# A transformer block: rounded keys and queries are stored once, and a pair's load takes them twice

## The chip, the cores and the metric

The kernel runs on one core of a Trainium2 chip. A core has five engines that run side by side, each through its own list of instructions: TensorE (PE, matrix products; PEld is its weight load), VectorE (DVE), ScalarE (ACT), GpSimd (POOL) and SyncE (SP). SP computes nothing: all transfers of this kernel are issued on it, in program order, and are carried out by the core's 16 DMA engines. The metric is the device time of one execution in microseconds (us), as the median of several runs. The profile comes from one more execution, taken by the hardware profiler.

## The reference

The block takes `x` (1 x 2048 x 512), modulates and normalizes it, and adds a gated attention over 32 heads of 16 columns and a gated dense layer with the Mish activation:

```python
mod = (_silu(c) @ w_mod).reshape(c.shape[0], 6, 1, -1)      # sa, ca, ga, sb, cb, gb
h = _layernorm(x) * (1 + ca) + sa
q, k, v = split(h @ wqkv)                                   # 32 heads, 16 columns each
p = softmax((q @ k.T) * 16 ** -0.5)                         # 2048 x 2048 a head
x = x + ga * (concat(p @ v) @ wo)
h = _layernorm(x) * (1 + cb) + sb
x = x + gb * (mish(h @ w1 + b1) @ w2)                       # 512 -> 1792 -> 512
```

All of it is in 32-bit floats.

## The kernel before

PE multiplies in a rounded 32-bit format. To keep the accuracy, a number is split into its rounded part (`qh`, called hi here) and the remainder (`ql`, lo), and a product is taken as hi x hi + hi x lo + lo x hi. For keys and queries this sum is folded into the contraction: 16 columns of a head become 48 rows, in which hi and lo stand in such an order that row by row the three products come out. A head's query rows are hi, hi, lo and its key rows hi, lo, hi, interleaved by column.

The rows are built through memory. `qk_unit` computes 128 columns (8 heads) of queries or keys for a block of 512 positions (`TB`), splits them, and its `put` (lines 266 to 277) stores them to the scratch tensors `qscr` (32 heads x 50 rows x 2048) and `kscr` (32 x 48 x 2048). Rounded rows are written twice there: queries by two transfers, keys by one transfer whose source repeats. Rows 48 and 49 of `qscr` start as zeros (`constants`, line 470) and are replaced in the loaded tile by the negated row maxima, split likewise (`mt`, line 577), so that the product subtracts the maximum.

Attention goes by *pairs* of heads. `load_q` (L313) and `load_k` (L322) bring one pair into one of five tiles `qa` and five tiles `ka`: head 0 into partitions 0 to 49, head 1 into 64 to 113, one transfer a head and operand. A *round* `n` handles 4 heads, pairs `2n` and `2n + 1`, for one block of 512 queries; there are 32 rounds of 16 steps. In each step PE takes products for the maxima of a later round (L539, reduced by DVE at L541), scores of this round (L588, exponentials by ACT at L591) and products with the values (L606), and in between a slice of other work: the projections early on, the dense layer of the block before later (L139). Before the rounds, maxima of the first rounds are taken at L553.

The order is written by hand. A step has two half-steps, and `at(h, f)` hangs a load or a store on half-step `h`. Loads of pairs:

```python
if n > 2: at(32 * (n - 2) + (2 if n in (3, 4, 5, 7) else 15 if n % 2 == 0 else 9), lambda n=n: load_pair(2 * n))
if n > 1: at(32 * (n - 1), lambda n=n: load_pair(2 * n + 1))
```

The maxima run 20 steps ahead of the scores (`PRO`), so the odd pair's tile is first read by L539 some 8 half-steps after its load is due. Its tile becomes free only when the scores that used it are done, which is what SP waits for there. `mt` is sent at half-step 26 of a round of 32, for the scores that begin 6 half-steps later.

SP signals the landing of its transfers on eight semaphores in turn (`DMAHW0` to `DMAHW7`). A transfer is issued only when the one eight places before it on the queue has landed, so at most eight are under way.

Of the kernel before, what the change touches and what calls it, by code (L numbers as in the profile page):

```python
# [8 lines left out]
F32 = mybir.dt.float32  # L9
# [9 lines left out]
def adaln_block(ctx: ExitStack, tc: tile.TileContext, x, wqkv, wo, w1, b1, w2, c, w_mod, out):  # L19
    nc = tc.nc  # L20
    P = 128
    S, D = x.shape[1], x.shape[2]
    F = w1.shape[1]
    H = 32
    DH = D // H
    DK = D // P
    FT = F // P
    TB = 512
# [25 lines left out]
    dram = ctx.enter_context(tc.tile_pool(name="dram", bufs=1, space=DRAM))  # L54
    ps = ctx.enter_context(tc.tile_pool(name="ps", bufs=1, space=PSUM))

    kscr = dram.tile([H, 48, S], F32, name="kscr")
    qscr = dram.tile([H, 50, S], F32, name="qscr")
    vscr = dram.tile([G, P, VROW], F32, name="vscr")
    woscr = dram.tile([DK, P, 2, D], F32, name="woscr")  # L60
    w1scr = dram.tile([FT, P, 2, D], F32, name="w1scr")
# [27 lines left out]
    def dap(t, off, ap):  # L89
        return bass.AP(tensor=t.tensor, offset=t.offset + off, ap=ap)  # L90

    def hi_copy(eng, hi, src):
        if eng == "a":
            nc.scalar.copy(hi, src)
        elif eng == "v":
            nc.vector.tensor_copy(hi, src)
        else:
            nc.gpsimd.tensor_scalar(hi, src, 1.0, 0.0, op0=ALU.mult, op1=ALU.add)  # L98

    def lo_sub(eng, lo, src, hi):  # L100
        (nc.gpsimd if eng == "p" else nc.vector).tensor_sub(lo, src, hi.bitcast(F32))  # L101
# [15 lines left out]
    def mm3(acc, ah, al, bh, bl, late="a"):  # L117

        n = len(ah)
        seq = ((ah, bh), (ah, bl), (al, bh)) if late == "a" else ((ah, bh), (al, bh), (ah, bl))  # L120
        seq = [(l[k], r[k]) for l, r in seq for k in range(n)]
        for i, (l, r) in enumerate(seq):
            mm(acc, l, r, i == 0, i == len(seq) - 1)
# [41 lines left out]
    def bank(tag="ms"):  # L165
        return ring() if tag == "ring" else ps.tile([P, TB], F32, tag=tag, name="bk", bufs=1)
# [25 lines left out]
    def clear(h):  # L192

        return h if h < 60 or h % 32 < 25 else h - h % 32 + 34
# [10 lines left out]
    def at(h, f):  # L205

        hooks.setdefault(h, []).append(f)
# [38 lines left out]
    def qk_unit(kind, ct, tb, tag):  # L246

        wh, wl = slices[kind, ct]
        acc = bank(tag)
        ts_ = slice(tb * TB, (tb + 1) * TB)  # L250
        mm3(acc, [wh[:, k, :] for k in range(DK)], [wl[:, k, :] for k in range(DK)],
            [h_h[:, k, ts_] for k in range(DK)], [h_l[:, k, ts_] for k in range(DK)], "b")

        def fin(h=None):
            qh = qp.tile([P, TB], F32R, tag="qh", name="qh", bufs=2)
            ql = qp.tile([P, TB], F32R, tag="ql", name="ql", bufs=2)
            if h is None:
                hi_copy("a", qh, acc)
                lo_sub("v", ql, acc, qh)
            else:  # L260
                qf = pw.tile([P, TB], F32, tag="raw", name="qf", bufs=1)
                nc.scalar.copy(qf, acc)  # L262
                hi_copy("p", qh, qf)
                lo_sub("p", ql, qf, qh)
            scr, rows = (qscr, 50) if kind == 0 else (kscr, 48)

            def put():
                put_away.add((kind, ct, tb))
                o = 8 * ct * rows * S + tb * TB
                if kind == 0:  # L270
                    for r, src in enumerate((qh, qh, ql)):
                        nc.sync.dma_start(dap(scr, o + r * S, [[rows * S, 8], [3 * S, DH], [1, TB]]), src.bitcast(F32))
                    return
                hi = qh.bitcast(F32)
                twice = bass.AP(tensor=hi.tensor, offset=hi.offset, ap=[list(hi.ap)[0], [0, 2], [1, TB]])
                nc.sync.dma_start(dap(scr, o, [[3 * S, P], [2 * S, 2], [1, TB]]), twice)
                nc.sync.dma_start(dap(scr, o + S, [[3 * S, P], [1, TB]]), ql.bitcast(F32))

            put() if h is None else at(clear(h + (5 if h > 60 else 2)), put)
        return fin  # L280
# [25 lines left out]
    def load_q(pp, rows=50):  # L306
        n, j = divmod(pp, 2)
        qb, g = divmod(n, G)
        h = 4 * g + 2 * j
        qt = qa[pp % NR].bitcast(F32)  # L310
        assert (0, h // 8, qb) in put_away, (pp, put_away)
        for s in range(2):
            nc.sync.dma_start(qt[64 * s:64 * s + rows, :], qscr[h + s, :rows, qb * TB:(qb + 1) * TB])  # L313

    def load_k(pp, tb=None):
        n, j = divmod(pp, 2)
        h = 4 * (n % G) + 2 * j
        kt = ka[pp % NR].bitcast(F32)
        at_ = slice(0, S) if tb is None else slice(tb * TB, (tb + 1) * TB)
        assert {(1, h // 8, i) for i in (range(NB) if tb is None else (tb,))} <= put_away, (pp, put_away)  # L320
        for s in range(2):
            nc.sync.dma_start(kt[64 * s:64 * s + 48, at_], kscr[h + s, :, at_])  # L322

    def load_pair(pp):
        load_q(pp)
        load_k(pp)


    with ExitStack() as es:
# [23 lines left out]
        zer = lp.tile([P, TB], F32, name="zer")  # L353
# [113 lines left out]
        apply_tb(1)  # L467
        def constants():
            for q4 in range(S // TB):
                nc.sync.dma_start(dap(qscr, 48 * S + q4 * TB, [[50 * S, H], [S, 2], [1, TB]]), zer[:64, :])  # L470
            nc.sync.dma_start(dap(vscr, VROW - 16, [[VROW, P], [P * VROW, G], [1, 16]]), zer[:, :16 * G])
            nc.sync.dma_start(b1c, b1.rearrange("(f p) -> p f", p=P))

        def unit(fin):
            pe_run()
            fin()

        constants()
        for tb in range(NB):
            if tb + 2 < NB:  # L480
# [27 lines left out]
            if tb == 0:  # L508
                for pp in range(2):
                    load_q(pp, 48)  # L510
            for pp in range(2):
                load_k(pp, tb)
# [7 lines left out]
    ap = ctx.enter_context(tc.tile_pool(name="ap", bufs=1, reuse_waits="tile"))  # L520
# [1029 lines left out]
```

## Time and profile before

| | |
|---|---|
| median of 3 runs | 1691.56 us (1690.99 to 1694.38) |
| the profiled execution | 1691.02 us, span 1689.2 us |
| PE busy | 1667.3 us |
| pair loads | 124 of keys, 384 KB each; 124 of queries, 100 KB each |
| DMA, mean | 141 GB/s, 238.98 MB |
| written to memory | 51.45 MB |

The span runs from the first instruction to the last. Times in rows are in us from the span's start, unless marked ns. In a row of a timeline stand start, duration, engine, line, operation, and what it writes and reads; `SPq` rows are the issuing of transfers, not their running. In a row of windows stand the stretch, its length, busy time of PE, PEld, DVE, ACT and POOL with counts of instructions, the clock granted to PE as a share, the mean busy share of the 16 DMA engines, and the GB/s that they moved.

### The profile page before, as it was taken

What the parts mean: (1) busy time and instruction counts of PE and PEld (TensorE: products, weight loads), DVE (VectorE), ACT (ScalarE), POOL (GpSimd) and SP (SyncE); (2) the same over time, 40 slices, a digit from 0 to 9 for tenths busy, and PEclk for the clock granted to TensorE, in tenths of its full rate; (3) what the DMA queues carried; (4) which work ended last, traced back from release to release, by engine and by line L of the source; (5) the groups of instructions that cost most, each with busy time, mean ns of one, the idle gap of its engine ahead of it and who ended that gap; (6) DMA issues with size and microseconds to landing.
All of it is one profiled execution on the core that took longest, in us unless ns stands there. A gap on an engine that the chain in (4) does not pass through costs nothing.

```text
span 1689.2 us, 33772 instructions
## 1 busy us (share of the span) xinstructions
PE 1667.3 (99%) x12418; PEld 921.5 (55%) x12418; DVE 1441.5 (85%) x2369; ACT 1355.1 (80%) x2612; POOL 821.1 (49%) x843
## 2 busy tenths in 40 slices
PE   7999999999999999999999999999999999999999
PEld 5755655555444455555555455555555455555687
DVE  8898888888989988888889888888889888883377
ACT  6257777777778998888888998888888998889674
POOL 7555224655313564556323564556323565555442
PEclk9999999999999999999999999999999999999999
DMA  7877556777755443434355434534354533533261
GB/s 248 269 244 199 147 150 185 218 223 216 231 142 146 110 94 98 117 88 129 84 137 152 115 77 93 139 77 127 87 144 122 130 94 77 144 107 132 75 230 63
DMA packets 115406, 238.98 MB, mean 141 GB/s; under 512 B 24928, under 2 KB 50544, under 8 KB 109288
## 3 DMA queue, kind: packets, MB, share of 16 engines
q1 hardware_dynamic: 115240, 236.82, 49.9%
q8 instruction: 98, 1.61, 0.4%
q14 instruction: 68, 0.56, 0.1%
HBM read 180.48 MB, written 51.45 MB: 137 GB/s over the span
## 4 chain that ended last, share of the span: by engine, by line
PE 91%; DVE 3%; ACT 3%; DMA 2%; POOL 1%; issue 1%; SPq 0%; ACTq 0%; DVEq 0%; POOLq 0%
PE bk L606 29%; PE ring L588 22%; PE ring L539 20%; PE bk L139 11%; PE bk L132 3%; PE ring L1219 2%; PE ring L132 2%; DVE mx L541 2%; ACT pr L591 1%; PE ring L553 0%; DMA qa<-mt 0%; DMA xt<-in_A_x 0%; PE ring L922 0%; DMA kscr<-qh 0%; PE ring L568 0%
## 5 line engine op out<-in xcount | busy, mean ns | idle before, releaser
L541 DVE TENSOR_REDUCE mx<-ring 128x1 f32<-128x512 f32 x1968 | 1223.1, 682 | 150.0 <-PE ring L539 136.4
L591 ACT ACTIVATE pr<-ring 128x512 f32<-128x512 f32 x2048 | 1078.4, 603 | 207.1 <-PE bk L139 124.7
L539 PE MATMUL ring<-ka,qa 64*128 64x512 f32 x1968 | 817.9, 429 | 1.4 <-ACT pr L591 1.1
L588 PE MATMUL ring<-qa,ka 64*128 64x512 f32 x2048 | 759.1, 402 | 3.4 <-ACT pr L591 1.9
L606 PE MATMUL bk<-pr,vg 128*32 128x512 f32 x4096 | 545.1, 604 | 0.0
L539 PEld LDWEIGHTS ring<-ka,qa 64*128 64x128 f32 x1968 | 350.5, 184 | 326.2 <-DVE mx L541 251.3
L588 PEld LDWEIGHTS ring<-qa,ka 64*128 64x128 f32 x2048 | 373.7, 184 | 194.7 <-DVE mx L541 111.4
L139 PE MATMUL bk<-h,w 64*128 64x512 f32 (+1 forms) x1080 | 278.1, 390 | 0.0
L139 PE MATMUL bk<-w,a_h 64*128 64x512 f32 x632 | 210.9, 413 | 0.0
L139 PEld LDWEIGHTS bk<-h,w 64*128 64x128 f32 x1080 | 178.5, 184 | 9.3 <-ACT pr L591 1.5
L606 PEld LDWEIGHTS bk<-pr,vg 128*32 128x32 f32 x4096 | 81.2, 108 | 135.4 <-issue 126.0
L139 PE MATMUL bk<-w,a_l 64*128 64x512 f32 x316 | 124.0, 392 | 0.0
L139 PEld LDWEIGHTS bk<-w,a_h 64*128 64x128 f32 x632 | 106.8, 184 | 4.3 <-ACT hb L800 1.0
L978 POOL TENSOR_TENSOR y<-yd,y 128x512 f32<-128x512 f32 x44 | 56.9, 1293 | 89.0 <-ACT yd L977 79.7
L812 POOL TENSOR_SCALAR qq<-ee 128x512 f32<-128x512 f32 x25 | 15.5, 619 | 169.6 <-ACT ee L806 169.6
L828 POOL TENSOR_TENSOR qq<-qq,rr 128x512 f32<-128x512 f32 x42 | 54.1, 1289 | 85.9 <-ACT rr L822 85.9
L814 POOL TENSOR_TENSOR hb<-hb,ee 128x512 f32<-128x512 f32 x42 | 54.1, 1288 | 79.6 <-DVE ee L810 77.7
L139 PE MATMUL bk<-w,o_hl 64*128 64x512 f32 x288 | 79.1, 405 | 0.0
L101 POOL TENSOR_TENSOR a_l<-hb,a_h 128x512 fp32r<-128x512 f32 x53 | 73.1, 1379 | 4.4
L98 POOL TENSOR_SCALAR qh<-qf 128x512 fp32r<-128x512 f32 x27 | 16.7, 619 | 90.8 <-ACT qf L262 69.4
L139 PEld LDWEIGHTS bk<-w,a_l 64*128 64x128 f32 x316 | 58.3, 185 | 3.4
L139 PE MATMUL bk<-h_h,wl 64*128 64x512 f32 x168 | 57.2, 420 | 0.2 <-ACT pr L591 0.2
(219 smaller groups left out, 1909.1 us busy)
## 6 DMA issues: line engine op xcount, KB each, us to landing
ka<-kscr SPq DMA_DIRECT2D x124, 384.0 KB
w<-w2scr SPq DMA_DIRECT2D x56, 512.0 KB
w<-w1scr SPq DMA_DIRECT2D x46, 512.0 KB
vg<-vscr SPq DMA_DIRECT2D x32, 552.0 KB
qa<-qscr SPq DMA_DIRECT2D x124, 100.0 KB
kscr<-qh SPq DMA_DIRECT2D x16, 512.0 KB
qscr<-qh SPq DMA_DIRECT2D x32, 256.0 KB
w2scr<-hl SPq DMA_DIRECT2D x14, 512.0 KB
```

The source lines that it names most:

```text
L101: (nc.gpsimd if eng == "p" else nc.vector).tensor_sub(lo, src, hi.bitcast(F32))
L132: nc.tensor.matmul(acc, l, r, start=start, stop=stop)
L139: i = nc.tensor.matmul(acc, l[64 * g:64 * g + 64], r[64 * g:64 * g + 64], start=start and not then, stop=bool(stop and then))
L539: nc.tensor.matmul(pm, qt[64 * s:64 * s + 64, qs * P:(qs + 1) * P], kt[64 * s:64 * s + 64, kb * TB:(kb + 1) * TB], start=True, stop=True)
L541: nc.vector.tensor_reduce(out=mxs[n][:, s, 4 * j + qs, kb:kb + 1], in_=pm, op=ALU.max, axis=AX.X)
L588: nc.tensor.matmul(p_, kt[64 * s:64 * s + 64, kc * P:(kc + 1) * P], qt[64 * s:64 * s + 64, :], start=True, stop=True)
L591: e = nc.scalar.activation(pr, p_, AF.Exp, scale=SCALE)
L606: nc.tensor.matmul(accs[n][32 * h:32 * h + 32, :], vgs[n][:, o:o + 32], pts.pop((t, h)), start=(kc == 0), stop=(kc == 15))
L814: (nc.vector if tail else nc.gpsimd).tensor_mul(hb, hb, ee)
L828: nc.gpsimd.tensor_mul(qq, qq, rr)
L978: nc.gpsimd.tensor_add(y[i], yd, y[i])
L1219: nc.tensor.matmul(po[i // 2][:, i % 2, :], l[:, s], w[:, r, :], start=(f == 0 and j == 0), stop=(f == FT - 1 and j == 2))
```

## The change

Three things change, all in transfers; no other engine's instructions differ.

- **Stores.** `kscr` has 32 rows a head and `qscr` 34: 16 rounded, 16 of the remainder, and for queries the two rows of zeros. Each of `qh` and `ql` is stored once, by one transfer. For queries one transfer of 256 KB goes (16 of them in all); for keys the first transfer shrinks from 512 KB to 256 KB. The memory side of both now counts 8 heads, 16 rows, 512 elements, where that of the keys counted 128 rows.
- **Loads.** The rounded rows are read twice by one transfer, whose source starts with a step of 0 and a count of 2; a second transfer brings the remainder (and for queries the two zero rows). A pair takes eight transfers in place of four.
- **Order of rows.** The rows of a tile are no longer interleaved: queries are 16 hi, 16 hi, 16 lo, keys 16 lo, 16 hi, 16 hi. The 48 products are the same, summed in another order.

```diff
-    kscr = dram.tile([H, 48, S], F32, name="kscr")
-    qscr = dram.tile([H, 50, S], F32, name="qscr")
+    kscr = dram.tile([H, 32, S], F32, name="kscr")
+    qscr = dram.tile([H, 34, S], F32, name="qscr")
...
-                if kind == 0:
-                    for r, src in enumerate((qh, qh, ql)):
-                        nc.sync.dma_start(dap(scr, o + r * S, [[rows * S, 8], [3 * S, DH], [1, TB]]), src.bitcast(F32))
-                    return
-                hi = qh.bitcast(F32)
-                twice = bass.AP(tensor=hi.tensor, offset=hi.offset, ap=[list(hi.ap)[0], [0, 2], [1, TB]])
-                nc.sync.dma_start(dap(scr, o, [[3 * S, P], [2 * S, 2], [1, TB]]), twice)
-                nc.sync.dma_start(dap(scr, o + S, [[3 * S, P], [1, TB]]), ql.bitcast(F32))
+                for r, src in enumerate((qh, ql)):
+                    nc.sync.dma_start(dap(scr, o + r * DH * S, [[rows * S, 8], [S, DH], [1, TB]]), src.bitcast(F32))
...
         for s in range(2):
-            nc.sync.dma_start(qt[64 * s:64 * s + rows, :], qscr[h + s, :rows, qb * TB:(qb + 1) * TB])
+            b, o = 64 * s, (h + s) * 34 * S + qb * TB
+            nc.sync.dma_start(qt[b:b + 32, :], dap(qscr, o, [[0, 2], [S, DH], [1, TB]]))
+            nc.sync.dma_start(qt[b + 32:b + rows, :], dap(qscr, o + DH * S, [[S, rows - 32], [1, TB]]))
...
         for s in range(2):
-            nc.sync.dma_start(kt[64 * s:64 * s + 48, at_], kscr[h + s, :, at_])
+            b, o = 64 * s, (h + s) * 32 * S + at_.start
+            nc.sync.dma_start(kt[b:b + DH, at_], dap(kscr, o + DH * S, [[S, DH], [1, w]]))
+            nc.sync.dma_start(kt[b + DH:b + 48, at_], dap(kscr, o, [[0, 2], [S, DH], [1, w]]))
```

On the SP queue this moves what stands behind a pair's load. First, a place in the middle of the rounds: the load of pair 25 (tiles `qa0`, `ka0`) with the transfers behind it, a weight (`w1`), the sums (`sm`) and the head rows (`od`) of the round just ended; the names in brackets are the semaphores waited for. Before:

```order
L313 DMA qa0_107<-qscr_67 50x512 [waits PE_49]
L313 DMA qa0_107<-qscr_67 50x512 [waits DMAHW2_49]
L322 DMA ka0_105<-kscr_66 48x2048 [waits DMAHW3_49]
L322 DMA ka0_105<-kscr_66 48x2048 [waits DMAHW4_49]
L751 DMA w1_7775<-w1scr_70 128x1024 [waits DMAHW5_49,PE_49]
L631 DMA sm_7773<-ot_7769 128x1x16 [waits DMAHW6_49,Activation_49]
L635 DMA od_7771<-ot_7769 16x512 [waits DMAHW7_49,Pool_49]
```

And with the change, at the same place:

```order
L308 DMA qa0_107<-qscr_67 32x1x512 [waits PE_49]
L309 DMA qa0_107<-qscr_67 18x512 [waits DMAHW2_49]
L308 DMA qa0_107<-qscr_67 32x1x512 [waits DMAHW3_49]
L309 DMA qa0_107<-qscr_67 18x512 [waits DMAHW4_49]
L319 DMA ka0_105<-kscr_66 16x2048 [waits DMAHW5_49]
L320 DMA ka0_105<-kscr_66 32x1x2048 [waits DMAHW6_49]
L319 DMA ka0_105<-kscr_66 16x2048 [waits DMAHW7_49]
L320 DMA ka0_105<-kscr_66 32x1x2048 [waits DMAHW0_49]
L749 DMA w1_7875<-w1scr_70 128x1024 [waits DMAHW1_49,PE_49]
L629 DMA sm_7873<-ot_7869 128x1x16 [waits DMAHW2_49,Activation_49]
```

A pair now takes all eight semaphores, and the weight behind it waits for the pair's own first transfer, `sm` for its second, where before they waited for transfers ahead of the pair.

Second, the start of the rounds, at the load of pair 3 (tiles `qa3`, `ka3`) between two stores of keys. Before:

```order
L276 DMA kscr_66<-qh_990 128x2x512 [waits DMAHW3_49,Pool_49]
L277 DMA kscr_66<-ql_991 128x512 [waits DMAHW4_49,Pool_49]
L313 DMA qa3_110<-qscr_67 50x512 [waits DMAHW5_49]
L313 DMA qa3_110<-qscr_67 50x512 [waits DMAHW6_49]
L322 DMA ka3_631<-kscr_66 48x2048 [waits DMAHW7_49]
L322 DMA ka3_631<-kscr_66 48x2048 [waits DMAHW0_49]
L276 DMA kscr_66<-qh_1011 128x2x512 [waits DMAHW1_49,Pool_49]
L277 DMA kscr_66<-ql_1012 128x512 [waits DMAHW2_49,Pool_49]
```

And with the change, where the first two stores (8x16x512 both) stand as before, from the load on:

```order
L308 DMA qa3_110<-qscr_67 32x1x512 [waits DMAHW3_49]
L309 DMA qa3_110<-qscr_67 18x512 [waits DMAHW4_49]
L308 DMA qa3_110<-qscr_67 32x1x512 [waits DMAHW5_49]
L309 DMA qa3_110<-qscr_67 18x512 [waits DMAHW6_49]
L319 DMA ka3_650<-kscr_66 16x2048 [waits DMAHW7_49]
L320 DMA ka3_650<-kscr_66 32x1x2048 [waits DMAHW0_49]
L319 DMA ka3_650<-kscr_66 16x2048 [waits DMAHW1_49]
L320 DMA ka3_650<-kscr_66 32x1x2048 [waits DMAHW2_49]
L271 DMA kscr_66<-qh_1033 8x16x512 [waits DMAHW3_49,Pool_49]
L271 DMA kscr_66<-ql_1034 8x16x512 [waits DMAHW4_49,Pool_49]
```

The stores behind the pair now wait for transfers of the pair itself. The whole SP queue grows from 1022 to 1274 transfers.

More of the change, by code (lines that the diff above doesn't have):

```diff
@@ L264, in fin @@
                 lo_sub("p", ql, qf, qh)
-            scr, rows = (qscr, 50) if kind == 0 else (kscr, 48)
+            scr, rows = (qscr, 34) if kind == 0 else (kscr, 32)
             def put():
@@ L318, in load_k @@
         kt = ka[pp % NR].bitcast(F32)
-        at_ = slice(0, S) if tb is None else slice(tb * TB, (tb + 1) * TB)
+        at_, w = (slice(0, S), S) if tb is None else (slice(tb * TB, (tb + 1) * TB), TB)
         assert {(1, h // 8, i) for i in (range(NB) if tb is None else (tb,))} <= put_away, (pp, put_away)
         for s in range(2):
-            nc.sync.dma_start(kt[64 * s:64 * s + 48, at_], kscr[h + s, :, at_])
+            b, o = 64 * s, (h + s) * 32 * S + at_.start
+            nc.sync.dma_start(kt[b:b + DH, at_], dap(kscr, o + DH * S, [[S, DH], [1, w]]))
+            nc.sync.dma_start(kt[b + DH:b + 48, at_], dap(kscr, o, [[0, 2], [S, DH], [1, w]]))
     def load_pair(pp):
@@ L469, in constants @@
             for q4 in range(S // TB):
-                nc.sync.dma_start(dap(qscr, 48 * S + q4 * TB, [[50 * S, H], [S, 2], [1, TB]]), zer[:64, :])
+                nc.sync.dma_start(dap(qscr, 32 * S + q4 * TB, [[34 * S, H], [S, 2], [1, TB]]), zer[:64, :])
             nc.sync.dma_start(dap(vscr, VROW - 16, [[VROW, P], [P * VROW, G], [1, 16]]), zer[:, :16 * G])
```

## The prediction

> **What bounds the kernel now.** I read the page's totals first, then the groups by line for what PE waits for, then the transfers' own rows.
>
> ```profile
> span 1689.2 us, 33772 instructions
> PE 1667.3 (99%) x12418; PEld 921.5 (55%) x12418; DVE 1441.5 (85%) x2369; ACT 1355.1 (80%) x2612; POOL 821.1 (49%) x843
> ...
> PE 91%; DVE 3%; ACT 3%; DMA 2%; POOL 1%; issue 1%; SPq 0%; ACTq 0%; DVEq 0%; POOLq 0%
> ```
>
> PE is never without work, and 91% of the chain that ended last is PE. An idle microsecond forced on PE is therefore a microsecond of time, less what PE now loses to slower partners anyway. The two groups that read the loaded keys and queries:
>
> ```profile
> L539 PE MATMUL ring<-ka,qa 64*128 64x512 f32 x1968 | 817.9, 429 | 1.4 <-ACT pr L591 1.1
> L588 PE MATMUL ring<-qa,ka 64*128 64x512 f32 x2048 | 759.1, 402 | 3.4 <-ACT pr L591 1.9 <-DMA qa<-mt 1.2
> ```
>
> For transfers PE waits 1.2 us in all (the last column names what ended its idle time). So the change can win nothing on PE, and the question is how much room each load has. The SP queue around two pair loads, and the first product on PE that reads the first of them:
>
> ```profile
> 606.20 2.77 SPq L577 DMA_DIRECT2D qa<-mt  x4
> 612.84 0.84 SPq L313 DMA_DIRECT2D qa<-qscr  x2
> 613.72 0.78 SPq L322 DMA_DIRECT2D ka<-kscr  x2
> 618.49 0.34 SPq L751 DMA_DIRECT2D w<-w1scr  x1
> ...
> 624.47 0.88 SPq L313 DMA_DIRECT2D qa<-qscr  x2
> ...
> 636.66 0.61 SPq L644 DMA_DIRECT2D rb<-rscr  x1
> ...
> 658.85 0.68 SPq L313 DMA_DIRECT2D qa<-qscr  x2
> ```
>
> ```profile
> 625.54 0.50 PE L539 MATMUL ring<-ka,qa 64*128 64x512 f32 x1
> ```
>
> This product is the 801st for the maxima; a pair has 32, so it is the first of pair 25, whose load starts at 612.84. The lead of this odd pair is 12.7 us. The next pair (624.47) is loaded for a later use and has about twice that. One round of two pairs takes 46.0 us (612.84 to 658.85).
>
> **How many DMA engines a transfer uses.** Share is of 16 engines, the last number GB/s.
>
> ```profile
> 12.00:15.00 3.00, 3.00 (x15) 2.22 (x11) 1.02 (x4) 2.08 (x4) 2.68 (x8) 1.00 1.08 397
> 33.00:35.00 2.00, 2.00 (x19) 2.00 (x18) 1.90 (x5) 0.86 (x3) 1.49 (x2) 1.00 0.52 190
> 612.00:614.00 2.00, 2.00 (x20) 0.82 (x16) 2.00 (x4) 1.99 (x4) 1.83 (x3) 1.00 0.07 20
> 615.00:620.20 5.20, 5.20 (x42) 2.75 (x40) 4.46 (x8) 4.37 (x10) 4.94 (x5) 1.00 0.99 171
> 637.70:638.00 0.30, 0.30 (x6) 0.26 (x4) 0.30 (x1) 0.30 (x1) 0.22 (x2) 1.00 0.00 0
> 638.50:639.00 0.50, 0.50 (x8) 0.16 (x8) 0.50 (x2) 0.50 (x2) 0.50 (x1) 1.00 0.26 86
> ```
>
> ```profile
> 30.41 1.35 SPq L272 DMA_DIRECT2D qscr<-qh  x2
> 31.86 0.60 SPq L272 DMA_DIRECT2D qscr<-ql  x1
> ```
>
> At 638.5 only `rb` moves (issued at 636.66), whose source counts 4 rows, then a repeat of 16, then 512 elements: share 0.26, four engines of 16. At 33 to 35 three query stores are outstanding together, whose destination counts 8 heads outermost: share 0.52, eight engines, and all three on the same eight. The key load at 615 counts 48 rows: 0.99. So the outermost count of either side bounds the engines, and a transfer of few engines does not find the idle ones. The changed loads of rounded parts read `[[0, 2], [S, 16], [1, w]]`: outermost count 2, as in `rb`'s form. I take two engines, the same two each time. An engine's rate is 397/16 = 24.8 GB/s at 12 us and 86/(0.26 x 16) = 20.7 at 638.5; I take 24.
>
> [...]
>
> **A pair's load, new.** For a head on each of the two engines: rounded keys 32 x 8 KB / 2 = 131,072 bytes, 5.46 us; rounded queries 32 x 2 KB / 2, 1.37 us; its remainders (16 rows over 16 engines, 18 over 9) 0.34 + 0.17 us. Sum 7.34, for two heads 14.7 us, plus 1.3 us from issue to first packet (636.66 to 638.0): 16.0 us, against 12.7 us of lead. All other engines are done long before. Eight issues in place of four add about 2 us of SP time a pair, some 250 x 0.4 = 100 us in all; they run beside the transfer and cost nothing of their own.
>
> **Stage 480 to 1510 us.** What else the two engines carry decides how far a load slips. Stages of the span, and what moved in two of them:
>
> ```profile
> 100.00:480.00 380.00, 376.07 (x3039) 203.60 (x3039) 333.43 (x557) 294.32 (x584) 173.46 (x165) 1.00 0.69 198
> 480.00:1510.00 1030.00, 1027.48 (x7844) 534.35 (x7841) 916.52 (x1550) 898.87 (x1748) 506.60 (x512) 1.00 0.43 111
> ```
>
> ```profile
> DMA packets 40455, 114.28 MB, mean 111 GB/s; under 512 B 12064, under 2 KB 12768, under 8 KB 36128
> ...
> ka<-kscr SPq DMA_DIRECT2D x88, 384.0 KB
> ...
> qa<-qscr SPq DMA_DIRECT2D x88, 100.0 KB
> ```
>
> Less keys (34.6 MB) and queries (9.0), 70.7 MB is other traffic, 4.4 MB an engine, 184 us of 1030: 0.18. A load is late by 16.0 - 12.7 = 3.3 us if nothing lies ahead of it, and by 14.7/0.82 + 1.3 - 12.7 = 6.5 if its share of the rest does. I take 4.5, nearer the low end, since at 612 to 614 the share is 0.07: the queue is empty when the load starts. PE gets about 1 us back, because it now waits for DVE in most steps, and DVE catches up while PE stands:
>
> ```profile
> PEld ring L539 <- DVE mx L541: 251.3, 303, 0.8
> ```
>
> 22 odd pairs (88 loads are 44 pairs) x 3.5 = **77 us** (2.3 to 5.5 each: 51 to 121). The even pair's load queues behind the odd one's: free at 612.84 + 16.0 = 628.9, landed about 643.6, 19 us after its issue. Most have over 22 us, a few 14 to 18: **10 us** (0 to 30).
>
> **Stage 100 to 480 us.** Here the stores run too.
>
> ```profile
> DMA packets 44394, 75.23 MB, mean 198 GB/s; under 512 B 6700, under 2 KB 23025, under 8 KB 42817
> ...
> ka<-kscr SPq DMA_DIRECT2D x32, 384.0 KB
> qscr<-qh SPq DMA_DIRECT2D x28, 256.0 KB
> ...
> kscr<-qh SPq DMA_DIRECT2D x9, 512.0 KB
> ```
>
> Less keys and queries 59.4 MB, 3.7 MB an engine if spread evenly. Query stores lie on eight engines, the change halves the rounded ones (14 x 256 KB less) and brings the key stores onto eight: about 4.1 MB on each of the first two, 171 us. Sixteen pairs x 14.7 are 235 us: together 406 us of work in 380 us. The removed stores are 0.46 MB an engine, 19 us, inside this count. So here the two engines are the bound, and what comes behind a load is late too. The maxima's 4 KB transfers have the least room:
>
> ```profile
> 309.41 0.68 SPq L313 DMA_DIRECT2D qa<-qscr  x2
> ...
> 325.25 3.21 SPq L577 DMA_DIRECT2D qa<-mt  x4
> ...
> 331.91 0.67 SPq L313 DMA_DIRECT2D qa<-qscr  x2
> ```
>
> The scores of the next round start when buffers fall free at 331.9. With 0.45 of the engines' time taken by the rest, the pair of 309.4 lands after 14.7/0.55 + 1.3 = 28 us, at 337.4, and the `mt` transfers (destination: 2 rows outermost) end behind it, 6 us late. 8 rounds x (3.5 + 6) = **76 us**; ends 26 (throughput alone) and 140 (5.5 + 12).
>
> **Before 100 us.** Between two stores of keys the chain runs through the SP queue:
>
> ```profile
> 86.75 1.30 POOL ql L101
> ...
> 88.84 1.32 SPq L313
> ...
> 92.58 7.33 DMA kscr<-qh
> ```
>
> A store behind a pair's load now is issued 2 us later and lands behind 14.7 us of work on its engines where the load took about 5.5: 11 us. Three pairs (71, 89 and 125 us) lie so: 33, and 4 us for the doubled first loads: **37 us** (10 to 60). After 1510 us no key is loaded: nothing.
>
> **Sum.** 77 + 10 + 76 + 37 = 200 us on the profiled execution's 1691.0 us: **1891 us**; the median of the runs, 1691.56, lies 0.5 us above it. Low ends give 87, 1778 us. At 20.7 GB/s a pair takes 18.3 us: 143 + 30 + 164 + 60, 2088 us.
>
> **Rival A, not slower.** The builder of the transfers spreads the rounded rows by their 32 destination rows over 16 engines. Then a pair's bytes and engines are those of today, it lands by 620.2 + 2 us, before 625.5, and PE does not see it; the removed stores save a few us around 86 to 100, the SP queue costs them again: 1688 to 1694 us. It decides if a load stays under 12.7 us. Against it: `rb` has 64 destination rows and yet four engines.
>
> **Rival B, far slower.** The key load at 615 moves only 171/16 = 10.7 GB/s an engine. If the rounded rows go at that pace, a head takes 12.2 us for keys, a pair 28 us, two pairs 56 of 46 us: the two engines need 62 x 28 + 177 MB / 16 / 24 = 2200 us, about 2250 with the ends. Against it: there sixteen engines write 48 rows at once, here two engines write 16 each, as `rb`'s four do at 20.7.
>
> [...]
>
> **Rival C, the loads alone.** The early stages absorb their lateness, and only odd pairs stall: 77 + 10, 1778 us, the low end.
>
> **Chances.** Forecast with its ends 0.80, A 0.05, B 0.07, C and less 0.08. Range 1778 to 2088. About 0.2% is what measurements here tell from no change: A splits into 0.02 faster and 0.03 same; the rest is slower, 0.95.
>
> **What would show it.** PE's idle column at the maxima's line names DMA `ka` or `qa`, 50 to 70 times, 3 to 6 us each; share near 2/16 in the windows after a pair load; `qa<-mt` on the chain before 480 us; fewer bytes written. Wrong if the share after a load stays near 1 (A), or stalls pass 10 us everywhere (B).

## The result: 21.5% slower, and the profile after

The changed kernel takes 2056.2 us (2050.1 to 2060.1, 5 runs) against 1692.0 (1691.0 to 1694.4, 5 runs): a ratio of 1.215, 95% interval 1.214 to 1.217. The forecast was 1891 us, range 1778 to 2088: the sign and the place were right, the size was short by 165 us. The profiled execution took 2050.1 us. From its page, the totals, the granted clock by slices of 51 us, the chain of waits and the two groups that read the loaded tiles:

```profile
span 2048.3 us, 34146 instructions
PE 1768.1 (86%) x12418; PEld 973.6 (48%) x12418; DVE 1451.8 (71%) x2369; ACT 1366.6 (67%) x2612; POOL 818.9 (40%) x843
...
PEclk9878889988998999999999999999999999999999
...
HBM read 180.48 MB, written 43.06 MB: 109 GB/s over the span
...
PE 54%; DMA 33%; SPq 6%; issue 2%; DVE 2%; ACT 2%; POOL 1%; ACTq 0%; POOLq 0%; DVEq 0%
...
L537 PE MATMUL ring<-ka,qa 64*128 64x512 f32 x1968 | 858.4, 448 | 192.3 <-DMA ka<-kscr 155.9
L586 PE MATMUL ring<-qa,ka 64*128 64x512 f32 x2048 | 792.5, 419 | 52.7 <-DVE mx L539 29.5
```

DMA was 2% of the chain and is 33%. Two things happened to PE, and the second line tells them apart. Its idle time went from 1689.2 - 1667.3 = 21.9 us to 280.2: **258.3 us of standing**. And the same 12418 products, busy for 1667.3 us before, are busy for 1768.1: **100.8 us of slower products**. Together 359.1 us, the whole difference of the spans (2048.3 - 1689.2). The forecast knew only the first kind. The stores did shrink, from 51.45 MB to 43.06 MB written.

How the loss grows, by counting PE's products from the start. Before, and after:

```profile
0.00:480.00 480.00, 464.74 (x3531) 268.66 (x3533) 420.15 (x665) 333.64 (x651) 234.93 (x251) 1.00 0.71 211
```

```profile
0.00:650.00 650.00, 511.97 (x3527) 292.48 (x3527) 424.22 (x665) 338.86 (x651) 234.37 (x251) 0.88 0.46 143
```

What was done by 480 us is now done by 650, so 170 us are lost by then (123 standing, 47 slower products) and 189 later (135.5 and 53.6). The first product of the scores starts at 145.7 us where it started at 101.9, so 44 of the 170 are lost ahead of the rounds.

What PE waits for, later and earlier than 650 us (time in all, times, longest):

```profile
PE ring L537 <- DMA ka<-kscr: 105.4, 23, 7.3
PE ring L537 <- issue: 25.1, 5, 5.3
```

```profile
PE ring L537 <- DMA ka<-kscr: 50.5, 12, 6.0
PE ring L586 <- DVE mx L539: 29.5, 4, 9.6
PE ring L586 <- DMA qa<-mt: 21.7, 2, 15.8
```

Now the pair followed in the prediction, number 25, on the SP queue:

```profile
801.68 0.60 SPq L308 DMA_DIRECT2D qa<-qscr  x1
802.33 0.44 SPq L309 DMA_DIRECT2D qa<-qscr  x1
...
804.30 0.59 SPq L320 DMA_DIRECT2D ka<-kscr  x1
...
805.40 0.59 SPq L320 DMA_DIRECT2D ka<-kscr  x1
...
810.55 4.75 SPq L633 DMA_DIRECT2D od<-ot  x4
815.41 0.66 SPq L308 DMA_DIRECT2D qa<-qscr  x1
820.13 0.28 SPq L309 DMA_DIRECT2D qa<-qscr  x1
```

SP itself tells when the loads land, because each issue needs the landing eight places before. The last of the four `od` is eight places behind the first load of rounded keys; taken alone, its issue starts at 814.79:

```profile
814.79 0.51 SPq L633 DMA_DIRECT2D od<-ot  x1
```

The last row of the list above it is eight places behind the second load and starts at 820.13. So the two land 13.1 and 18.4 us after the pair's first issue, 5.3 us apart. On PE, in the same stretch (in brackets the wait ahead of a product and what ended it):

```profile
813.08 0.40 PE L537 MATMUL ring<-ka,qa 64*128 64x512 f32 x1
820.20 0.76 PE L537 MATMUL ring<-ka,qa 64*128 64x512 f32 x1 [5.73 <-DMA ka<-kscr]
...
822.47 0.62 PE L586 MATMUL ring<-qa,ka 64*128 64x512 f32 x1
...
825.06 0.39 PE L586 MATMUL ring<-qa,ka 64*128 64x512 f32 x1
```

PE stands for 5.7 us, and then the first products take 0.62 us each where the same products take 0.39 ahead of the wait and again from 825 on. The windows around it (the eighth column is the granted clock, the ninth the DMA share) say why:

```profile
804.00:810.00 6.00, 6.00 (x50) 3.54 (x47) 5.23 (x10) 5.17 (x12) 5.66 (x6) 1.00 0.53 146
815.00:820.00 5.00, 0.00 (x0) 0.00 (x0) 0.00 (x0) 0.00 (x0) 3.72 (x4) 0.72 0.16 57
820.00:822.00 2.00, 1.80 (x8) 1.61 (x10) 0.83 (x2) 0.57 (x1) 0.00 (x0) 0.50 0.20 65
825.00:828.00 3.00, 3.00 (x26) 1.65 (x26) 2.48 (x4) 2.51 (x5) 0.32 (x1) 1.00 0.14 37
```

While PE stands, the DMA share is 0.16 (two engines of 16 are 0.125), and the clock falls. It was 1.00 from 804 to 810; in the trace's clock records it is 0.50 from 817.2 to 824.0, so for 3.8 us after PE has its data at 820.2, and 1.00 again from there. The wait of 5.7 us was enough for that; the last section counts what goes ahead of such a fall.

That the slower products are the clock's doing can be counted. In the trace's clock records the granted clock is 1.00 or 0.50 and nothing between, and the stretches at 0.50 add up to 325 us. PE is busy in 198 us of them. If it did this work twice as fast at full clock, 99 us would be saved: an estimate, against the 100.8 us measured.

### The profile page after: what moved, and what is told of

It reads as the page before. It is cut to its first block, busy times and chain, and to the rows that moved or that the text cites. A ratio compares the mean times of both kernels' runs of the same rounds, so it can differ in the third digit from the quotient of the medians.

```text
span 2048.3 us, 34146 instructions
## 1 busy us (share of the span) xinstructions
PE 1768.1 (86%) x12418; PEld 973.6 (48%) x12418; DVE 1451.8 (71%) x2369; ACT 1366.6 (67%) x2612; POOL 818.9 (40%) x843
## 3 DMA queue, kind: packets, MB, share of 16 engines
HBM read 180.48 MB, written 43.06 MB: 109 GB/s over the span
## 4 chain that ended last, share of the span: by engine, by line
PE 54%; DMA 33%; SPq 6%; issue 2%; DVE 2%; ACT 2%; POOL 1%; ACTq 0%; POOLq 0%; DVEq 0%
DMA ka<-kscr 22%; PE bk L604 16%; PE ring L586 13%; PE ring L537 12%; PE bk L139 6%; DMA sm<-ot 3%; PE bk L132 2%; PE ring L1217 2%; PE ring L132 2%; SPq L309 2%; SPq L308 2%; DMA qa<-qscr 1%; SPq L319 1%; DMA y<-in_A_x 1%; SPq L320 1%
## 5 line engine op out<-in xcount | busy, mean ns | idle before, releaser
L589 ACT ACTIVATE pr<-ring 128x512 f32<-128x512 f32 x2048 | 1090.1, 602 | 494.5 <-PE bk L139 332.1
L537 PE MATMUL ring<-ka,qa 64*128 64x512 f32 x1968 | 858.4, 448 | 192.3 <-DMA ka<-kscr 155.9
L586 PE MATMUL ring<-qa,ka 64*128 64x512 f32 x2048 | 792.5, 419 | 52.7 <-DVE mx L539 29.5
L537 PEld LDWEIGHTS ring<-ka,qa 64*128 64x128 f32 x1968 | 371.7, 194 | 538.5 <-DVE mx L539 234.1
L604 PE MATMUL bk<-pr,vg 128*32 128x512 f32 x4096 | 566.9, 627 | 0.0
L586 PEld LDWEIGHTS ring<-qa,ka 64*128 64x128 f32 x2048 | 394.5, 194 | 249.6 <-DVE mx L539 144.7
L139 PE MATMUL bk<-h,w 64*128 64x512 f32 (+1 forms) x1080 | 287.9, 401 | 0.6 <-DMA w<-w1scr 0.6
L139 PE MATMUL bk<-w,a_h 64*128 64x512 f32 x632 | 223.2, 434 | 0.0
L553 DVE TENSOR_REDUCE mx<-ring 128x2 f32<-128x1024 f32 x40 | 46.9, 1219 | 24.5 <-PE ring L551 24.0
```

The source lines that it names most:

```text
L139: i = nc.tensor.matmul(acc, l[64 * g:64 * g + 64], r[64 * g:64 * g + 64], start=start and not then, stop=bool(stop and then))
L537: nc.tensor.matmul(pm, qt[64 * s:64 * s + 64, qs * P:(qs + 1) * P], kt[64 * s:64 * s + 64, kb * TB:(kb + 1) * TB], start=True, stop=True)
L553: nc.vector.tensor_reduce(out=mxs[n][:, :, jq, kb:kb + 1], in_=pm, op=ALU.max, axis=AX.X)
L586: nc.tensor.matmul(p_, kt[64 * s:64 * s + 64, kc * P:(kc + 1) * P], qt[64 * s:64 * s + 64, :], start=True, stop=True)
L589: e = nc.scalar.activation(pr, p_, AF.Exp, scale=SCALE)
L604: nc.tensor.matmul(accs[n][32 * h:32 * h + 32, :], vgs[n][:, o:o + 32], pts.pop((t, h)), start=(kc == 0), stop=(kc == 15))
```

## The experiments

Times are medians; the kernel before ran beside each group at 1691.0 to 1691.8 us. Theory at the outset: the rounded rows ride on two DMA engines because the outermost count of their source is 2; the pair so lands later than its lead; each wait also costs clock. Rivals: the number of transfers and their waits on SP; the stores; the repeat itself.

### The same rows without the count of 2

First, no repeat at all (queries alike):

```diff
-            nc.sync.dma_start(kt[b + DH:b + 48, at_], dap(kscr, o, [[0, 2], [S, DH], [1, w]]))
+            for r in range(1, 3):
+                nc.sync.dma_start(kt[b + DH * r:b + DH * r + DH, at_], dap(kscr, o, [[S, DH], [1, w]]))
```

> The changed kernel, but each load of rounded rows is two plain transfers of 16 rows, each over 16 engines, in place of one that repeats its source: 12 transfers a pair in place of 8, the same bytes, stores as in the change. Theory (two engines carry the rounded rows): the stalls go, 1690 to 1705 us; 62 late transfers of SP time do not reach PE. Rival (the number of issues and their waits on eight semaphores is the cause): more issues, so at least the 2056 us of the change, up to 2150. Rival (stores on eight engines matter): 50 us and more above the kernel before stay in the part ahead of 480 us.

Second, the repeat moved inside, with queries stored as hi and lo by turns so that the rows of both tiles still match:

```diff
-            nc.sync.dma_start(kt[b + DH:b + 48, at_], dap(kscr, o, [[0, 2], [S, DH], [1, w]]))
+            nc.sync.dma_start(kt[b:b + 32, at_], dap(kscr, o, [[S, DH], [0, 2], [1, w]]))
...
+            nc.sync.dma_start(qt[b:b + 32, :], dap(qscr, o, [[S, 32], [1, TB]]))
+            nc.sync.dma_start(qt[b + 32:b + rows, :], dap(qscr, o, [[2 * S, rows - 32], [1, TB]]))
```

> The change with the repeat moved inside: keys are loaded from 16 rows, each repeated twice, so the outermost count of the source is 16 and not 2; queries lie in memory as hi and lo by turns and are loaded as 32 rows and then every second row. Eight transfers a pair, stores once, as in the change; the sum of the 48 products is the same. Theory (engine count): 1686 to 1698 us, level with the kernel before or a little under it. Rival (eight issues a pair instead of four): about the 2056 us of the change.

Measured: **1721.7** (1.018, 1.016 to 1.019) and **1711.0 us** (1.012, 1.010 to 1.013). Of the 364 us, 334 and 345 are gone, with 12 and with 8 transfers a pair and with the stores of the change. They came out 17 and 13 us over the range expected, so something else costs 19 to 30 us (below).

Third and fourth, the run without repeats, but the source counted in twos or in fours from the outside:

```diff
-                nc.sync.dma_start(kt[...], dap(kscr, o, [[S, DH], [1, w]]))
+                nc.sync.dma_start(kt[...], dap(kscr, o, [[S, 2], [2 * S, 8], [1, w]]))
```

> The run without repeats (two plain transfers of 16 rounded rows each), but the memory side of each is written with an outermost count of 2, then 8 (every second row, then the others); 12 transfers a pair as there, nothing repeated. In this run and its twin with 4, the rounded rows stand in another order than the remainders, so the two small corrections of the product pair wrong columns; the work is the same. Theory (outermost count sets the engines): back to the time of the change or more, 2040 to 2110 us, since the queue adds issues. Rival (the repeat, a step of 0, is what is slow): 1722 us as without repeats.

> The same with an outermost count of 4, then 4. Theory (four engines carry half as much each; the last key transfer is issued 5.3 us after the first of the pair and needs 2.2 + 2.7 us more, 10.2 in all, under the 12.7 us of lead): no stall at the odd pairs after 480 us, 1722 to 1760 us. If time went evenly with bytes an engine: about half of the loss of two engines, 1850 to 1900.

Measured: **2081.4** with an outermost count of 2 (1.233, 1.230 to 1.236) and **1830.2 us** with 4 (1.083, 1.081 to 1.085). The count alone, with nothing repeated, brings the whole loss back, so it is neither the step of 0 nor the number of transfers. Counts of 2, 4 and 16 give 2081, 1830 and 1722 us. A count of 4 was expected to be enough and was not. After 560 us PE still waited there, though mostly for a short time:

```profile
PE ring L539 <- DMA ka<-kscr: 18.2, 8, 5.2
PE ring L588 <- DMA qa<-mt: 5.8, 1, 5.8
PE ring L539 <- DMA od<-ot: 4.5, 5, 1.0
```

The larger part of its loss lies earlier: 3485 products are done by 580 us, which before took less than 480.

### Keys or queries

> The change with the outermost repeat kept for keys only; rounded queries come by two plain transfers of 16 rows. The two engines then carry 10.9 us a pair in place of 13.6, so a pair that came 5.3 us late comes about 2.6 us late. Theory: 22 stalls of 2 to 3 us in the stage from 480 to 1510 us, many too short for the clock to fall; mean granted clock 0.97 or more; 1790 to 1880 us. If the clock falls after every stall whatever its length: 1880 to 1930. If queries and not keys make the load late: 1700 or less.

> The change with the outermost repeat kept for queries only; rounded keys come by two plain transfers of 16 rows over 16 engines (ten transfers a pair). The two engines then carry only the rounded queries, 32 KB each a head. Theory: a pair is in well before its 12.7 us are over, so no stalls after 480 us; what is left is the price of the added issues early on, between the 19 us of eight and the 30 us of twelve transfers, and some lateness of the maxima's small transfers: 1712 to 1730 us. Rival (small rows on two engines are the slow part): 1800 or more.

Measured: **2004.5** with the repeat in front for the keys (1.186, 1.184 to 1.188), **1764.9 us** with it for the queries (1.041, 1.036 to 1.045). Both are above their ranges. With keys alone the load is a little shorter than with both:

```profile
782.48 0.79 SPq L309 DMA_DIRECT2D qa<-qscr  x2
...
786.36 0.62 SPq L321 DMA_DIRECT2D ka<-kscr  x1
...
799.29 0.31 SPq L309 DMA_DIRECT2D qa<-qscr  x1
```

The last row waits for the second load of rounded keys and starts 16.8 us after the pair's first issue, against 18.4 with both. So 1.6 us came off, where the expectation had taken off the queries' 2.7 us in full, and the load is still 4 us over its lead. A reason that fits, but is not shown, is that the keys could not have run at once: their first rounded load goes out behind six transfers of queries in place of four, 2.8 us after the pair's first issue (2.6 with both). With queries alone little is lost after 480 us (PE busy 1019 of the 1030 us to 1510, against 1027 before, clock 1.00). Of the 43 us over the run without repeats, 39 are lost by the product that the kernel before reaches at 480 us: the first scores start at 135.5 us in place of 127.9, and PE waits for `mt`, 9.5 us at the longest.

### The eight issues alone

The kernel before, with its four transfers a pair cut in two:

```diff
-            nc.sync.dma_start(kt[64 * s:64 * s + 48, at_], kscr[h + s, :, at_])
+            for lo, hi in ((0, 32), (32, 48)):
+                nc.sync.dma_start(kt[64 * s + lo:64 * s + hi, at_], kscr[h + s, lo:hi, at_])
```

> The kernel before, stores and order of rows as there, with each load of keys and queries cut in two (rows 0 to 31 and the rest): eight transfers a pair in place of four, the same bytes, all of them over 9 to 16 engines. Theory (what is left with the repeat inside, 19 us, is SP's time for the added issues in the first 130 us): 1706 to 1714. Rival (it is the stores of keys on eight engines): 1690 to 1695.

Measured: **1708.1 us** (1.011, 1.009 to 1.012), 17 of the 19 us. Most of it is the start: there the two first pairs are loaded block by block, and weights (`wr`) stand behind these loads on SP. The last load of blocks and the weight in the kernel before, then in the split one:

```profile
58.59 1.99 SPq L322 DMA_DIRECT2D ka<-kscr  x4
60.63 0.45 SPq L234 DMA_DIRECT2D wr<-in_A_wqkv  x1
```

```profile
65.55 3.55 SPq L324 DMA_DIRECT2D ka<-kscr  x8
69.15 0.42 SPq L234 DMA_DIRECT2D wr<-in_A_wqkv  x1
```

Each block's load holds SP for 1.6 us more, and waits for stores add to that; the weight is 8.5 us late. With the repeat inside, it goes out at 76.4, and PE waits 6.8 us for the split weight (`wl`). The first scores start at 101.9 us before, 109.3 split, 117.6 with the repeat inside, 127.9 with twelve transfers, 145.7 in the changed kernel. By the 600th product on PE, 116 us into the kernel before, the profiled execution with split loads has lost 10.5 of its 15.2 us; another 4.5 follow by the products that the kernel before takes from 336 to 480 us, and their cause is open.

### Lateness without two engines

The run with the repeat inside, in which no pair load has an outermost count under 16, with the odd pair's load hung later from round 10 on:

```diff
-            at(32 * (n - 1), lambda n=n: load_pair(2 * n + 1))
+            at(32 * (n - 1) + (6 if n > 9 else 0), lambda n=n: load_pair(2 * n + 1))
```

> The run with the repeat inside (16 engines, 1711 us), but from round 10 on the odd pair's load is hung six half-steps later on the queue, behind the sums and head rows. There it would be issued about 11.3 us later (642.6 for 631.3), lands some 8 us after that, and is needed at 643.9. Theory (a stall is load time less lead, whichever engines carry it, and a stall of this length halves the clock): 22 stalls of 6 to 7 us, and some 2 us of slower products behind each: 1850 to 1930 us, mean granted clock 0.93 to 0.97. Rival (two busy engines, not lateness, do the harm): under 1750.

> The same with four half-steps: the load goes in behind a weight, ahead of the sums, about 6 us later than without, and comes 1 to 2 us late. Theory (a short stall leaves the clock alone): 22 stalls of 1 to 2 us, clock 0.98 or more, 1735 to 1765 us. If any stall halved the clock: mean clock 0.96 or less and 1775 to 1800.

Measured: **1924.8 us** with six half-steps (1.137, 1.136 to 1.139) and **1724.5** with four (1.019, 1.018 to 1.021). The first is in its range, mean clock 0.947:

```profile
span 1922.0 us, 34140 instructions
PE 1725.4 (90%) x12418; PEld 951.9 (50%) x12418; DVE 1446.4 (75%) x2369; ACT 1360.5 (71%) x2612; POOL 819.6 (43%) x843
...
PE ring L538 <- DMA ka<-kscr: 125.1, 26, 11.0
PE ring L538 <- DMA qa<-qscr: 37.0, 6, 9.0
```

Waits of 162 us and products slower by 50.5 us (1725.4 less 1674.9 without the shift) make 212.6 of the 212.9 us between the two spans. PE is busy in 114 us at half clock here, so the same estimate as above gives 57 for the 50.5. This is the picture of the changed kernel with no pair load of an outermost count of 2: what hurts is that a load ends after its lead. The second, below its range of 1735 to 1765, was to be 1 to 2 us late and was almost never late (7.9 us of waits for transfers and issues at the maxima after 500 us, mean clock 0.992). It shows how sharp the edge is, but what a short wait does to the clock it leaves open (see the last section).

### The price of the clock

The changed kernel, with products of no use put where PE stands (12, then 24 in place of 12, then 20 from round 9 on):

```diff
             pm = ring()
+            if (j, qs, s, kb) == (1, 0, 1, 0):
+                k0, q0 = ka[2 * n % NR], qa[2 * n % NR]
+                for _ in range(12):
+                    nc.tensor.matmul(pm, q0[64:, :P], k0[64:, :TB], start=True, stop=True)
```

> The change, with 12 more products on PE right ahead of the first product of each odd pair from the second round on (30 x 12). They repeat a product of the even pair into the bank that the next product overwrites, so their results are not used; they take some 5 us in which PE of the changed kernel stands. Theory (part of the loss is the clock, halved after a stall): PE no longer stands there, the mean granted clock rises from 0.92 to 0.95 or more and the time falls by 30 to 60 us, to 1996 to 2026, although 155 us of work are added. Rival (products are slow for another reason, such as transfers that write to the same memory): 2056 or more, and the clock stays.

> The run with 12 added products ahead of each odd pair's first product, with 24 in their place. The 12 took 3.0 us (819.07 to 822.07) and left 2.4 us of waiting, in which the clock still fell. 24 take 6.0 us and cover the wait. Theory (the clock falls because PE stands, and costs some 2 us each time): no wait for keys at the maxima from 480 us on, mean granted clock 0.97 or more, 1990 to 2025 us. Rival (the lateness alone sets the time and the clock costs nothing): 2045 to 2080.

> The change with 20 added products ahead of each odd pair's first one, from round 9 on only (23 x 20, 0.25 us each, 5.0 us a round), where the waits were 5.3 us long. The 24 of every round had overshot: they brought PE's other work down by 57 us and its idle time plus their own up by 50. Theory: most of the clock's price of these rounds, 23 x 2 us, comes back: 2005 to 2035 us, mean granted clock 0.95 to 0.97. Rival (the clock's price comes back elsewhere as waiting): 2045 or more.

Measured: **2050.4** with 12 (1.212, 1.209 to 1.215; clock 0.935), **2041.8** with 24 (1.207, 1.204 to 1.209; 0.958), **2030.7 us** with 20 late (1.201, 1.199 to 1.202; 0.947). The first two missed their ranges, the third is inside. The first can't be told from the changed kernel (2044.1 to 2055.4 against 2050.1 to 2060.1 us). Twelve took 3.0 us and not 5, so PE still stood for 2.4 us, and the clock still fell, as the 0.63 us shows:

```profile
819.07 3.01 PE L540 MATMUL ring<-ka,qa 64*128 64x512 f32 x12
824.52 0.79 PE L541 MATMUL ring<-ka,qa 64*128 64x512 f32 x1 [2.44 <-DMA ka<-kscr]
...
825.54 0.63 PE L541 MATMUL ring<-ka,qa 64*128 64x512 f32 x1
```

With 24:

```profile
span 2041.0 us, 35650 instructions
PE 1895.4 (93%) x13162; PEld 1092.2 (54%) x13162; DVE 1446.4 (71%) x2369; ACT 1362.3 (67%) x2612; POOL 821.2 (40%) x843
...
L540 PE MATMUL ring<-ka,qa 64*128 64x512 f32 x744 | 184.3, 402 | 0.0
```

PE's own products take 1895.4 - 184.3 = 1711.1 us, 57.0 less than in the changed kernel. But idle time and filler together are 329.9 us where it stood for 280.2, so 49.7 go again: 24 products are longer than many of the waits. With 20 from round 9 on the same sum is 31.1 won (of the 46 expected) and 11.0 lost, and the spans differ by just that, 20.1 us; the medians differ by 25.5. With 20 late (2030.0 to 2031.6 us) the kernel is faster than without by work that does nothing, so the clock's share is a cost of its own. How much of the 100.8 us an exact cover would win stays open.

None of these runs beats the kernel before. The two nearest both issue eight transfers a pair, the split loads with the old stores at 1708 us and the repeat inside with the smaller ones at 1711, so storing less won nothing in a kernel whose PE already works 99% of the time.

## Why the prediction was right in kind and short in size

**Two engines for a load with outermost count 2.** Right, and now shown: from 817.0 to 819.3 us, in the wait above, the share is 0.12 at 50 GB/s (two of 16 are 0.125), and plain rows in twos take 2081 us, in sixteens 1722. Rival A (spread over 16 engines) is out, and so is B (10.7 GB/s an engine): two loads of keys land 5.3 us apart, 131,072 bytes an engine in that time or 24.5 GB/s, close to the 24 taken. Rival C, that the early stages absorb their lateness, is out with 170 us lost by 480.

**A pair's load, 16.0 us.** It measured 18.4. The keys' term was good (5.3 us from the first landing to the second, so 10.7 for two, against 10.9). Short was what comes ahead of them: 1.3 us to the first packet, 2.7 for queries and 1.0 for remainders are 5.0, and it took 7.7. That 18 rows of a remainder ride on 9 engines, as the 1.0 has it, no run shows by itself; from 803.3 to 803.7 us of the changed kernel 14 packets of 2 KB and 7 small ones start, which would be two rows on each of seven engines. Where the 2.7 us go is open. The issues may have a part (the second load of rounded keys is issued 3.7 us after the first transfer of the pair), and so may the weight issued behind the pair at 807.35, which moves while the keys are not yet in (DMA share 0.93 and 0.80 from 808 to 810). That eight issues "cost nothing of their own" failed for certain at the start, where the split loads alone cost 17 us.

**Stage 480 to 1510, 77 + 10 us.** Lost: 189. PE stands 136 us more than before, in 28 waits of 4.7 us at the maxima, most of them for odd pairs as forecast. 22 waits of 3.5 net became 28 of 4.7, in accord with a load that is 2.4 us longer. The 1 us that DVE was to give back in each stall is not seen: the row it was read from is the weight load's wait, not that of the products, and over the whole span it only fell from 251.3 to 234.1 us; PE's products had 2.5 us of idle time in this stage to give (1030 less 1027.5). The other 53.6 us are the clock, which has no term in the sum at all: this is the step that failed. "An idle microsecond forced on PE is a microsecond of time" is where it went wrong; late in this kernel 136 us of standing cost 189.

**Stage 100 to 480, 76 us.** Lost: 126. The waits for `mt` and for keys are there (15.8 and 6.0 us at the longest). That the two engines are busy throughout, as the sum of 406 us has it, no row here shows; nor does one show that they are among the eight of the stores, which its 171 us take for granted. What the runs show in place of both is the 126. Again the clock is missing (0.88 up to 650, with products slower by 47 us, 10 of them ahead of the rounds), and the 6 us for each `mt` were too even: two long waits, and others that the profile puts down to DVE.

**Before 100, 37 us.** 44 measured, but for another reason in good part. I put it on stores landing behind loads on two engines. Split loads alone delay the first scores by 7 us, the repeat inside by 16, twelve transfers by 26: some 16 us come with eight issues and the new stores, without a repeat in front. The rest, some 28, comes with the repeat in front. How the 16 divide between issues and stores is not shown beyond the 7 of the split loads.

**After 1510: nothing.** Right: the first kernel's last score starts at 1585.1, now at 1943.8, 358.7 later, and the ends differ by 359.1.

**The range.** That 2056 us lies inside the range at all is in part luck: its high end, 2088, came from a pair of 18.3 us at a slower 20.7 GB/s an engine. The pair did take 18.4, but with engines at 24.5, and the 101 us of slower products stood in no term.

**What would show it.** PE's idle column at the maxima's line does name DMA `ka`, for 155.9 of 192.3 us, with up to 7.3 us a wait, but in 35 waits and not 50 to 70; the share in a wait is 0.16; `mt` is waited for before 480; bytes written fell. Nothing in that list would have shown the clock, which was quoted as 1.00 in every window of the kernel before.

## What to carry to other kernels

Read the outermost count of both sides of each transfer before costing it: a repeat belongs inside, where the kernel took 1711 us, and not in front, where it took 2056 and a late load moved at a DMA share of 0.12. For a late load compare the whole of its path (issues on the queue, start, bytes an engine) with its lead, since little is lost up to the edge and much behind it: two half-steps on the queue made 1925 us of 1724. And where PE is the bound, price a wait of several microseconds at more than its length: here 258 us of standing brought 101 us of slower products.

## What was not expected of the hardware

In the changed kernel's trace the clock is cut in steps of one length. Each stretch at 0.50, but for one cut off by the end of the records, is 3.41 us long or a multiple of it, and all of them lie on one grid of 3.41 us. The clock's falls go with how long PE is busy in a stretch of this grid. At full clock, PE was busy for less than half of the time in 42 stretches, and the next was at half clock after each of them; of 7 with 50 to 60%, 2 were followed by half clock, and of 449 with more, none. So here PE did not have to stand for a whole stretch. The wait of 5.7 us on this grid (first number behind the comma: PE's busy time; eighth column: the clock):

```profile
813.80:817.20 3.40, 0.67 (x8) 0.00 (x0) 0.78 (x2) 1.20 (x3) 1.95 (x3) 1.00 0.19 61
817.20:820.60 3.40, 0.40 (x2) 0.43 (x4) 0.00 (x0) 0.00 (x0) 1.77 (x2) 0.50 0.12 49
```

Two waits of 1.5 and 2.3 us in the changed kernel left the clock alone. The first leaves PE busy for 1.92 of 3.40 us, and the second is divided between two stretches:

```profile
902.50:905.90 3.40, 1.92 (x14) 1.30 (x14) 2.13 (x4) 1.65 (x4) 3.24 (x4) 1.00 0.03 10
1011.80:1015.20 3.40, 1.81 (x13) 1.16 (x13) 2.13 (x4) 0.81 (x2) 3.24 (x4) 1.00 0.06 22
1015.20:1018.60 3.40, 2.68 (x20) 1.29 (x21) 1.39 (x3) 3.35 (x8) 2.56 (x3) 1.00 0.01 2
```

The wait of 2.4 us behind 12 added products does not fit this count. There PE is busy for 2.58 of 3.40 us, and the clock falls all the same:

```profile
819.50:822.90 3.40, 2.58 (x12) 1.75 (x10) 0.00 (x0) 0.17 (x1) 2.98 (x3) 1.00 0.17 59
822.90:826.30 3.40, 1.78 (x8) 1.50 (x10) 0.79 (x2) 0.52 (x1) 0.78 (x2) 0.50 0.16 57
```

In this stretch PE runs almost nothing but added products, so these may count for less than the mix that they stand in for; no run here tests that.
